# Attention and a two-layer MLP on one core: the second matrix product by one level of Strassen's scheme on 12 of 16 inner blocks, with its weight decoded earlier

## The chip, the core and the metric

The kernel runs on one core of a Trainium2 chip. The metric is the device time of one launch in microseconds (us). In the text, PE is the matrix engine (TensorE), PEld its weight loads, DVE is VectorE, ACT is ScalarE, POOL is GpSimd, and SP is the engine from whose queue nearly every DMA is issued. Every engine takes its own instructions strictly in order; an instruction that waits holds up all that stand behind it on its engine.

## What is computed

Causal attention with 4 batches, 12 heads, 448 positions and head dimension 64, then an MLP on 1792 tokens of width 768, with 2048 inner features:

```python
scores = scale * q @ k.T                      # q, k, v: (4, 12, 448, 64) float32
scores = where(triu(ones, k=1), -1e9, scores)
p = exp(scores - max); p = p / (sum(p) + 1e-9)
x = (p @ v).transpose(0, 2, 1, 3).reshape(1792, 768)
h = x @ w_in                                  # first product, (768, 2048)
g = where(h >= 1, h, where(h <= -1, 0, (h + 1) ** 2 / 4))
out = g @ w_out                               # second product, (2048, 768)
```

The two weights arrive as 64-bit floats. The kernel sees them as pairs of 32-bit words and rebuilds float32 numbers from them.

## The kernel before

All work is entered as tasks of a list (`Plan`), each with one engine or several to choose from, its costs, and the buffers that it reads and writes. `Plan.solve` (L145) orders the PE tasks by nominal times that the program gives them, derives due times for all others, and runs a greedy schedule over nine pairs of settings and five rounds each; the best of them is written out as the instruction order of each engine. So a change in the tasks moves instructions on every engine, and the order on each engine is fixed when the program is built.

Numbers are carried as two parts: a rounded part ("hi") and the rest ("lo"). One product is three matmuls, hi by hi, hi by lo and lo by hi (`PASSES`, L479).

**Weights.** `decode` (L429) brings a block of 128 rows and 384 numbers in: one DMA of 384 KB into a staging tile, one ACT pass over the high words (L449), two DVE passes that put the float together (L452, L454), then the hi part as a copy (ACT, POOL or DVE, L413 and L415) and the lo part as a subtraction (POOL or DVE, L423 and L422). Each of the 16 slices f of a weight has two such blocks, called halves here. `w_in` is decoded while the first pairs of heads go through attention, `w_out` when the tiles of `w_in` come free, from 373 us on.

**Attention.** 24 pairs of heads follow one another (`prep_pair`, `prep_v`, `pair`): loads of q and k, a transpose on DVE (L577), scores on PE, minimum and exponential on DVE and ACT (L718, L722), transposes on PE (L657), and the product with v (L747). Matmuls of the first product (`mlp1`, L481) for the batch before are woven in between, 20 steps in each of the first four pairs of a batch, few in the fifth and none in the sixth.

**First product.** `mlp1` takes 18 matmuls of 448 columns for one slice of 128 inner features and one batch, then one ACT pass (L497), two DVE passes (L500, L506) for the function g, and a store into the DRAM scratch `g_scratch` (L510). After the last pair of heads only these matmuls are left for PE, from 373 to 420 us.

**Second product.** `TILES` (L330) cuts the 14 blocks of 128 tokens into groups of 4, 4, 3, 2 and 1. For each group the loop over the 16 slices f loads g back (`gr`), splits it into hi and lo (`gs`, ACT L413 and DVE L422), and issues for each token block six matmuls of 384 columns (L836): 3 passes by 2 halves of the output. 14 blocks x 16 slices x 6 are 1344 matmuls. The sums stay in PSUM (`a` with 5 buffers, `h` with 3) until the last slice, and are then copied out (L851, L855) and stored.

```python
both = [(c, m) for m in range(3) for c in range(2)]
nc.tensor.matmul(out=acc[t, c][:, :NO], lhsT=gs[:, a, (t - t0) * P:(t - t0 + 1) * P],
                 rhs=wo[f][:, z, c * NO:(c + 1) * NO], ...)
```

Of the kernel before, what the change touches and what calls it, by code (L numbers as in the profile page):

```python
# [303 lines left out]
def kernel(  # L304
# [9 lines left out]
    nc = tc.nc  # L314
# [15 lines left out]
    TILES = (4, 4, 3, 2, 1)  # L330
    GT = max(TILES)
# [13 lines left out]
        "w": KF, "st": 2, "wm": 2, "x": 9, "r": 3, "vv": 1, "h": 3,  # L345
# [3 lines left out]
        "gr": 4, "gs": 4, "ot": 2, "a": 5,  # L349
# [31 lines left out]
    mask2 = const.tile([P, 3 * P], F32, name="mask2")  # L381
# [6 lines left out]
    for i in range(NI):  # L388
        e = const.tile([P, P * (i // 2 + 1)], F32, name=f"e{i}")
        if i % 2 == 0:  # L390
            nc.gpsimd.memset(e[:, T * (i + 1):], 0.0)
        es.append(e)
    qb = [const.tile([P, 2, 2, T], F32R, name=f"qb{n}") for n in range(2)]
    zero = const.tile([P, 512], F32R, name="zero")
# [34 lines left out]
    def decode(w, c, src, prio, no):  # L429

        if no < 2 * (KF - NSTG):
            st, z = stages[no // 2 % NSTG], no % 2
            raw = lambda: st.tile.bitcast(U32)[:, z]
        else:
            st, z = buf("st", [P, 2 * S]), 0
            raw = lambda: st.tile.bitcast(U32)[:, :DM]
        m = buf("wm", [P, W2])

        def words(t):
            return raw().rearrange("p (c t) -> p c t", t=2)[:, :, t]  # L440

        def mu():
            return m.tile.bitcast(U32)

        hi = lambda: w[:, 0, c * W2:(c + 1) * W2]
        lo = lambda: w[:, 1, c * W2:(c + 1) * W2]
        dst, ap = src
        dma_task(lambda: dst(raw()), lambda: ap, dma(P * DM * 4), 0.38, writes=[(st, (z, 0)), (st, (z, 1))] + ([] if z or st in stages else [(w, ("to", c))]))
        task([("ACT", act(W2, 0.04), lambda: nc.scalar.activation(  # L449
            out=m.tile, in_=words(1).bitcast(F32), func=ACTF.Prelu, scale=W_SHIFT, alpha=W_SIGN))],  # L450
            prio, reads=[(st, (z, 1))], writes=[(m, 0)])
        task([("DVE", dve(W2, True), lambda: nc.vector.tensor_scalar(  # L452
            out=mu(), in0=mu(), scalar1=3, scalar2=None, op0=ALU.logical_shift_left), True)], prio, writes=[(m, 0)])
        task([("DVE", dve(W2) + 0.08, lambda: nc.vector.scalar_tensor_tensor(  # L454
            out=mu(), in0=words(0), scalar=29, in1=mu(), op0=ALU.logical_shift_right, op1=ALU.bitwise_or), True)],
            prio, reads=[(st, (z, 0))], writes=[(m, 0)])
        task(copy_alts(hi, lambda: m.tile, W2, "ACT POOL DVE"), prio, reads=[(m, 0)], writes=[(w, (0, c))])
        task(sub_alts(lo, lambda: m.tile, lambda: hi().bitcast(F32), W2, "POOL DVE"),
             prio, reads=[(m, 0), (w, (0, c))], writes=[(w, (1, c))])
# [4 lines left out]
    def load_w_in(f, prio):  # L464
        w = wi[f] = buf("w", [P, 2, DM], F32R)
        for c in range(2):
            src = w_in[c * K2 * P:(c + 1) * K2 * P, f * 2 * P:(f + 1) * 2 * P]
            decode(w, c, (lambda t: t.rearrange("p (k c) -> p k c", k=K2),
                          src.rearrange("(k p) c -> p k c", p=P)), prio, 2 * f + c)

    def load_w_out(f, prio):
        w = wo[f] = buf("w", [P, 2, DM], F32R)
        for c in range(2):
            decode(w, c, (lambda t: t, w_out[f * P:(f + 1) * P, c * DM:(c + 1) * DM]), prio, 2 * KF)
# [422 lines left out]
```

## Time and profile before

| What | Value |
|---|---|
| median of three timed runs | 659.58 us (658.79 to 660.16) |
| span of the profiled execution, first to last instruction | 657.8 us (no other time of that execution is given) |
| mean granted PE clock | 0.997 of full |
| PE busy | 637.1 us, 97% |
| DVE, ACT, POOL busy | 343.5, 334.9, 183.0 us |
| chain that ended last | PE 79%, DMA 8%, DVE 5%, ACT 3% |
| matmuls of the first product | 1152, of the second 1344 |

A row of the engine groups gives the engine, the operation, the tiles, the count, the busy time, the mean duration in ns, and then the idle time just before. Matmul durations overlap, so the spacing of starts in the timeline tells the rate of PE, not the mean duration.

### The profile page before, as it was taken

What the parts mean: (1) busy time and instruction counts of PE and PEld (TensorE: products, weight loads), DVE (VectorE), ACT (ScalarE), POOL (GpSimd) and SP (SyncE); (2) the same over time, 40 slices, a digit from 0 to 9 for tenths busy, and PEclk for the clock granted to TensorE, in tenths of its full rate; (3) what the DMA queues carried; (4) which work ended last, traced back from release to release, by engine and by line L of the source; (5) the groups of instructions that cost most, each with busy time, mean ns of one, the idle gap of its engine ahead of it and who ended that gap; (6) DMA issues with size and microseconds to landing.
All of it is one profiled execution on the core that took longest, in us unless ns stands there. A gap on an engine that the chain in (4) does not pass through costs nothing.

```text
span 657.8 us, 11550 instructions
## 1 busy us (share of the span) xinstructions
PE 637.1 (97%) x3782; PEld 558.6 (85%) x3782; DVE 343.5 (52%) x857; ACT 334.9 (51%) x877; POOL 183.0 (28%) x322
## 2 busy tenths in 40 slices
PE   7989999999898999999999999999999999999997
PEld 3447798887697888798887699999999999999997
DVE  4867787867666565665644476655532112112221
ACT  3879979757746556846555533444431112112122
POOL 3657665443412222612212133334310000000000
PEclk8999999999999999999999999999999999999999
DMA  9889999677776655756442465666642214213221
GB/s 220 227 240 228 234 264 275 190 214 204 195 230 187 168 148 154 180 171 178 101 128 62 156 214 159 199 195 195 196 160 65 64 49 145 73 49 109 72 84 49
DMA packets 91900, 105.75 MB, mean 161 GB/s; under 512 B 34368, under 2 KB 75840, under 8 KB 91840
## 3 DMA queue, kind: packets, MB, share of 16 engines
q1 hardware_dynamic: 91600, 104.46, 57.2%
q10 hardware_dynamic: 240, 0.55, 0.4%
q8 instruction: 30, 0.49, 0.3%
q14 instruction: 30, 0.25, 0.2%
HBM read 67.35 MB, written 20.19 MB: 133 GB/s over the span
## 4 chain that ended last, share of the span: by engine, by line
PE 79%; DMA 8%; DVE 5%; ACT 3%; SPq 2%; issue 2%; POOL 1%; DVEq 0%; ACTq 0%; POOLq 0%
PE h L488 29%; PE a L836 27%; PE h L836 9%; PE t L657 5%; PE t L747 4%; DMA st<-in_k_dram 4%; PE s L700 3%; SPq L405 2%; DMA st<-in_q_dram 2%; PE s L695 1%; DVE qs L577 1%; ACT e L722 1%; PE s L704 1%; DVE s L718 1%; DMA w<-in_moe_w_in_dram 1%
## 5 line engine op out<-in xcount | busy, mean ns | idle before, releaser
L488 PE MATMUL h<-x,w 128*128 128x448 f32 x1152 | 264.4, 372 | 2.2 <-DVE x L422 1.0
L488 PEld LDWEIGHTS h<-x,w 128*128 128x128 f32 x1152 | 208.5, 188 | 19.1 <-DVE x L422 2.2
L836 PE MATMUL a<-w,gs 128*128 128x384 f32 x1008 | 197.7, 334 | 0.0
L836 PEld LDWEIGHTS a<-w,gs 128*128 128x128 f32 x1008 | 176.8, 188 | 0.1
L422 DVE TENSOR_TENSOR gs<-gr,gs 128x512 fp32r<-128x512 f32 (+3 forms) x79 | 45.3, 574 | 139.3 <-ACT gs L413 135.1
L413 ACT ACTIVATE gs<-gr 128x512 fp32r<-128x512 f32 (+3 forms) x78 | 38.8, 500 | 137.4 <-PE h L836 103.5
L722 ACT ACTIVATE e<-s,mn 128x256 f32<-128x256 f32 (+6 forms) x168 | 80.8, 485 | 35.7 <-DVE mn L718 33.3
L718 DVE CUSTOM_DVE_ANT_0 s<-s,mask 128x256 f32<-128x256 f32 (+6 forms) x168 | 73.2, 453 | 45.8 <-PE s L700 22.7
L423 POOL TENSOR_TENSOR w<-wm,w 128x384 fp32r<-128x384 f32 x64 | 67.3, 1052 | 65.3 <-ACT w L413 64.0
L836 PE MATMUL h<-w,gs 128*128 128x384 f32 x336 | 80.7, 334 | 0.0
L657 PE MATMUL t<-ident,e 128*128 128x128 f32 x384 | 61.9, 279 | 5.7 <-DVE x L422 4.1
L679 ACT ACTIVATE pt<-t 128x512 f32<-128x512 f32 (+2 forms) x138 | 59.9, 466 | 4.4 <-PE t L657 3.1
L642 POOL TENSOR_SCALAR e<-e,su 128x256 f32<-128x256 f32 (+6 forms) x92 | 51.9, 569 | 35.3 <-DVE su L733 29.3
L657 PEld LDWEIGHTS t<-ident,e 128*128 128x128 f32 x384 | 44.1, 140 | 20.6 <-issue 5.8
L836 PEld LDWEIGHTS h<-w,gs 128*128 128x128 f32 x336 | 60.3, 188 | 0.0
L500 DVE TENSOR_TENSOR vv<-h,r 128x448 f32<-128x448 f32 x64 | 39.7, 620 | 36.4 <-ACT r L497 35.7
L497 ACT ACTIVATE r<-h,half 128x448 f32<-128x448 f32 x64 | 40.0, 632 | 36.2 <-PE h L488 35.4
L577 DVE STREAM_TRANSPOSE qs<-st 128x448 f32<-128x448 f32 x48 | 45.8, 966 | 22.1 <-DMA st<-in_q_dram 12.4
L747 PE MATMUL t<-pt,vr 128*64 128x448 f32 (+3 forms) x384 | 50.3, 391 | 0.6 <-ACT pt L679 0.6
L728 POOL TENSOR_SCALAR su<-su 128x2 f32<-128x2 f32 (+1 forms) x72 | 19.5, 270 | 107.9 <-ACT e L722 106.0
L747 PEld LDWEIGHTS t<-pt,vr 128*64 128x64 f32 (+1 forms) x384 | 23.2, 135 | 30.9 <-issue 21.5
L506 DVE SCALAR_TENSOR_TENSOR r<-r,vv 128x448 f32<-128x448 f32 x64 | 45.5, 711 | 1.3
(54 smaller groups left out, 506.4 us busy)
## 6 DMA issues: line engine op xcount, KB each, us to landing
g_scratch<-r SPq DMA_DIRECT2D x64, 224.0 KB, 2.4
st<-in_moe_w_out_dram SPq DMA_DIRECT2D x32, 384.0 KB, 3.4
w<-in_moe_w_in_dram SPq DMA_DIRECT2D x28, 384.0 KB, 4.8
st<-in_k_dram SPq DMA_DIRECT2D x94, 108.0 KB, 3.0
st<-in_q_dram SPq DMA_DIRECT2D x93, 108.0 KB, 3.0
q<-tt SPq DMA_DIRECT2D x76, 128.0 KB, 2.4
gr<-g_scratch SPq DMA_DIRECT2D x32, 256.0 KB, 2.7
k<-ks SPq DMA_DIRECT2D x76, 96.0 KB, 2.2
```

Of the source, the lines that this page charges most:

```text
L422: "DVE": ("DVE", dve(n), lambda: nc.vector.tensor_tensor(out=dst(), in0=x(), in1=y(), op=op), port),
L423: "POOL": ("POOL", pool_tt(n), lambda: nc.gpsimd.tensor_tensor(out=dst(), in0=x(), in1=y(), op=op), True),
L488: nc.tensor.matmul(out=h[:, :S], lhsT=wi[f][:, a, kk * P:(kk + 1) * P], rhs=x[:, c], start=(kk == 0 and n == 0), stop=(kk == KD - 1 and n ...
L506: task([("DVE", dve(S), lambda: nc.vector.scalar_tensor_tensor(out=r.tile, in0=r.tile, scalar=1.0, in1=y.tile, op0=ALU.min, op1=ALU.mult), ...
L577: task([("DVE", 0.81, lambda g=g, t=t: nc.vector.transpose(out=x[:, g].rearrange("p (r c) -> p c r", c=C), in_=t.tile.rearrange("p (c d) - ...
L642: ("POOL", pool_ts(n, 0.09), lambda: nc.gpsimd.tensor_scalar(out=ev(), in0=ev(), scalar1=sc(), scalar2=1.0, op0=ALU.mult, op1=ALU.mult), T ...
L657: nc.tensor.transpose(t[:, c:c + P], es[i][:, j * P:(j + 1) * P], ident)
L679: task([("ACT", act(n), lambda: nc.scalar.activation(out=dst(), in_=src(), func=ACTF.Copy)), ("DVE", dve(n), lambda: nc.vector.tensor_copy ...
L718: task([("DVE", dve(n) + 0.01, lambda s=s, n=n, i=i: nc.vector.tensor_tensor_reduce(out=s[:, :n], in0=s[:, :n], in1=mask2[:, 3 * P - n:] i ...
L722: task([("ACT", act(n, 0.19), lambda s=s, n=n, i=i: nc.scalar.activation(out=es[i][:, :n], in_=s[:, :n], func=ACTF.Exp, scale=-1.0, bias=m ...
L747: nc.tensor.matmul(out=o[64 * g:64 * g + 64, j * P:S], lhsT=vr[:k, j, g, :], rhs=pt[:k, 7 * j:5 * j + NI, g, :], start=(j == 0), stop=(j = ...
L836: nc.tensor.matmul(out=acc[t, c][:, :NO], lhsT=gs[:, a, (t - t0) * P:(t - t0 + 1) * P], rhs=wo[f][:, z, c * NO:(c + 1) * NO], start=(f == ...
```

## The change

**Second product.** The tokens are now taken in 7 pairs of blocks (`token_pair`), the inner slices in 8 pairs. For the first two pairs of slices (four slices, "plain") everything is as before: 8 products of three matmuls for a pair. For the other six pairs, a 2 x 2 by 2 x 2 block product is made with 7 products in place of 8 (Winograd's form of Strassen's scheme). That needs four sums of 128 x 128 blocks of g for each token pair (`sums`), hi and lo of 7 blocks in place of 4, and on the weight's side 7 tiles of hi and lo ("units") in place of 4, with four differences of halves (`minus`), once for the whole kernel. The 8 sums in PSUM (all 8 banks, 5 in `a`, 3 in `h`) are combined on the way out: one copy, nine additions, two stores of 384 KB; the last token pair does the plain slices last and stores four quarters of 192 KB.

**Weight.** The halves of slices 0 to 11 of `w_out`, 24 in all, are decoded during attention, from the eighth pair of heads on, two behind each pair, and parked as float32 in a DRAM scratch `w_scratch` by a store of 192 KB each. From 373 us on they are loaded from there, and only the 8 halves of slices 12 to 15 are still decoded then. 50 units are made, each with one hi copy and one lo subtraction.

**Buffers.** Constants of attention lie in a pool that closes with it; the weight tiles are units of half the size (32 in `w`, 9 in `w2` that opens after attention, 9 in `w3` that opens after the last store of g); the zero tile of the filling matmuls is a buffer of `k2`.

```diff
-    def decode(w, c, src, prio, no):
+    def decode(m, raw, src, writes=(), behind=(), after=()):
...
+    def narrow_w_out(f, c, behind):
+        m = small("wm", buf)
+        raw_out(f, c, m, raw_in(buf("sr", [P, DM])), behind=behind)
+        dma_task(lambda: w_dram[f, c], m[2], dma(P * W2 * 4), 0.35, reads=[m[:2]], writes=[(wkeys, (f, c))])
+
+    def out_half(f, c, m, units):
+        claim = [(u, "to") for u in units]
+        after = last + (tails if any(u.tag == "w3" for u in units) else [])
+        if f >= NARROW:
+            raw_out(f, c, m, raw_in(buf("st", [P, 2 * S])), claim, after=after)
+        else:
+            dma_task(m[2], lambda: w_dram[f, c], dma(P * W2 * 4), 0.35, reads=[(wkeys, (f, c))],
+                     writes=[m[:2]] + claim, after=after)
...
+    def load_w_out_pair(f):
...
+        out_half(f, 0, m11, [w["11"]])
+        split(m11, w["11"])
+        out_half(f, 1, m12, [w["T1"], w["T3"]])
+        minus(m12, m11, m11)
+        split(m11, w["T1"])
+        out_half(f + 1, 1, m22, [w["22"], w["T2"]])
+        minus(m22, m12, m12)
+        split(m12, w["T3"])
+        split(m22, w["22"])
+        minus(m22, m11, m22)
+        split(m22, w["T2"])
+        out_half(f + 1, 0, m21, [w["21"], w["T4"]])
+        split(m21, w["21"])
+        minus(m21, m22, m21)
+        split(m21, w["T4"])
...
+    for n in range(2 * NARROW):
+        narrow_w_out(n // 2, n % 2, [attn_tasks[7 + n // 2]])
...
+        def product(x, z, lhsT, unit, reads):
...
+                for n, (a, c) in enumerate(PASSES):
+                    nc.tensor.matmul(out=acc[x][:, :NO], lhsT=lhsT(a), rhs=unit[:, c],
+                                     start=(start and n == 0), stop=(stop and n == 2))
...
+        def sums(z):
+            for x, y, d, op in ((1, 3, 4, ALU.add), (0, 1, 1, ALU.subtract), (4, 0, 5, ALU.subtract), (2, 5, 6, ALU.subtract)):
...
+        for f, fast in groups:
+            z, hl = bbuf("z", [P, 7 * P]), bbuf("hl", [P, 2, 7 * P], F32R)
...
+            if fast:
+                for x in ORDER:
+                    i, name = BLOCK[x]
+                    product(x, z, lambda a, hl=hl, i=i: hl[:, a, i * P:(i + 1) * P], wo[f][name], both)
...
+        take("1", "1a")
+        add("6", "1a", "2a")
+        add("2", "1a", "1a")
+        add("3", "2a", "1b")
...
+        store(0, 0, DM, [0, 1])
+        store(1, 0, DM, [0, 1])
```

Lines move: the ACT pass of the decode is L446, the DVE passes L449 and L451, hi copies L418 and L420, lo and differences L427 and L428, matmuls of the first product L565, of the second L950.

Three places show how the order of the instructions moves. A row is line, operation, out<-in tiles, shape, and how many follow one another.

PE, the turn from the first product to the second, before (a and h are PSUM sums, w the weight, gs the split g):

```order
L488 MATMUL h<-x,w 128x448 x237
L836 MATMUL a<-w,gs 128x384 x6
L488 MATMUL h<-x,w 128x448 x3
L836 MATMUL a<-w,gs 128x384 x6
L488 MATMUL h<-x,w 128x448 x3
L836 MATMUL a<-w,gs 128x384
```

The same engine in the change, from the end of the first token pair on (w_5583 to w_5609 are units of the last pair of slices, w_4811 to w_4888 are plain units that the second token pair takes):

```order
L950 MATMUL a<-w_5489,hl 128x384 x3
L950 MATMUL h<-w_5528,hl 128x384 x3
L950 MATMUL a<-w_5583,hl 128x384 x3
L950 MATMUL h<-w_5529,hl 128x384 x3
L950 MATMUL h<-w_5584,hl 128x384 x3
L950 MATMUL a<-w_5608,hl 128x384 x3
L950 MATMUL a<-w_4811,hl 128x384 x3
L950 MATMUL a<-w_4813,hl 128x384 x3
L950 MATMUL a<-w_4821,hl 128x384 x3
L950 MATMUL a<-w_4826,hl 128x384 x3
L950 MATMUL a<-w_4888,hl 128x384 x3
L950 MATMUL a<-w_5609,hl 128x384 x3
```

The run of 237 matmuls before the turn is still there with the same length; the product with the last unit, w_5609, now stands behind five products of the next token pair.

DVE just after attention, before (wm is the decoded half, vv and r belong to the function g, gs is g split):

```order
L500 TENSOR_TENSOR vv<-h,r 128x448
L506 SCALAR_TENSOR_TENSOR r<-r,vv 128x448
L422 TENSOR_TENSOR gs<-gr,gs 128x512
L452 TENSOR_SCALAR wm<-wm 128x384
L454 SCALAR_TENSOR_TENSOR wm<-st,wm 128x384
```

DVE in the change, the last rows ahead of that last unit (sr, wm and st hold halves, hl the split g, ot the output):

```order
L427 TENSOR_TENSOR w_5529<-wm,w_5529 128x384
L427 TENSOR_TENSOR w_5584<-sr,w_5584 128x384
L427 TENSOR_TENSOR w_5608<-sr,w_5608 128x384
L427 TENSOR_TENSOR hl<-z,hl 128x512
L427 TENSOR_TENSOR ot<-h,ot 128x384
L427 TENSOR_TENSOR ot<-a,ot 128x384 x2
L427 TENSOR_TENSOR ot<-h,ot 128x384 x2
L427 TENSOR_TENSOR w_5609<-sr,w_5609 128x384
```

Lo parts that POOL made before are now mostly on DVE, and the last lo part of a unit stands behind the first output additions.

SP during the third batch of attention, before (st takes q and k, tt and ks are copies of them, r is g):

```order
L405 DMA st<-in_q_dram 32x864
L405 DMA g_scratch<-r 128x448
L405 DMA st<-in_k_dram 32x864 x4
L405 DMA g_scratch<-r 128x448 x2
L405 DMA q_3780<-tt 64x2x256 x4
L405 DMA g_scratch<-r 128x448
```

SP in the change at the same place:

```order
L410 DMA st<-in_q_dram 32x864
L410 DMA g_scratch<-r 128x448
L410 DMA st<-in_k_dram 32x864 x4
L410 DMA sr<-in_moe_w_out_dram 128x768
L410 DMA w_scratch<-wm 128x384
L410 DMA g_scratch<-r 128x448 x2
L410 DMA sr<-in_moe_w_out_dram 128x768
L410 DMA q_3891<-tt 64x2x256 x4
L410 DMA g_scratch<-r 128x448
L410 DMA k_3918<-ks 64x384 x4
L410 DMA w_scratch<-wm 128x384
```

A load of a raw half and the store of the decoded half stand in the queue between the loads of attention; in 18 of the 24 cases the store is the very next DMA behind its own load.

## Rows read from the trace of the kernel before

**Rows 1.** Page, part 1: busy us, share of the span, instructions of PE.
```profile
PE 637.1 (97%) x3782; PEld 558.6 (85%) x3782; DVE 343.5 (52%) x857; ACT 334.9 (51%) x877; POOL 183.0 (28%) x322
```

**Rows 2.** Windows: us, busy of PE, PEld, DVE, ACT, POOL; granted clock, DMA share, GB/s.
```profile
373.00:420.00 47.00, 47.00 (x232) 43.62 (x233) 34.06 (x55) 19.44 (x36) 17.61 (x19) 1.00 0.63 190
420.00:450.00 30.00, 30.00 (x173) 29.90 (x173) 17.25 (x30) 13.71 (x26) 9.94 (x11) 1.00 0.63 191
450.00:654.00 204.00, 203.68 (x1176) 203.36 (x1174) 55.08 (x104) 49.38 (x103) 11.89 (x12) 1.00 0.31 97
```

**Rows 3.** Timeline of PE in the second product: start, us, what.
```profile
419.29 1.23 PE L836 MATMUL a<-w,gs 128*128 128x384 f32 x6
...
449.68 2.41 PE L836 MATMUL a<-w,gs 128*128 128x384 f32 x13
451.93 0.33 PE L836 MATMUL h<-w,gs 128*128 128x384 f32 x1
```

**Rows 4.** The chain of waits, its longest piece: start, us, what.
```profile
372.98 46.47 PE h L488 x228
```

**Rows 5.** Windows of attention, columns as in rows 2.
```profile
70.00:110.00 40.00, 39.46 (x235) 33.44 (x234) 30.87 (x80) 32.16 (x84) 22.77 (x35) 1.00 0.99 265
...
190.00:208.00 18.00, 16.54 (x97) 13.54 (x95) 12.20 (x32) 8.90 (x25) 2.94 (x8) 1.00 0.81 223
...
172.00:373.00 201.00, 196.99 (x1209) 162.90 (x1207) 113.60 (x315) 119.89 (x339) 52.12 (x114) 1.00 0.59 158
```

**Rows 6.** The decode's second DVE pass from 70 to 110 us: count, duration.
```profile
L454 DVE SCALAR_TENSOR_TENSOR wm<-w,wm x10: 541/550/823, 81.3 to 108.7; 128x384 uint32<-128x384 uint32 x10
```

**Rows 7.** Groups by shape over the span: busy, mean ns, idle before and its releaser.
```profile
L422 DVE TENSOR_TENSOR gs<-gr,gs 128x384 fp32r<-128x384 f32 x16 | 8.9, 558 | 42.4 <-ACT gs L413 42.4
L422 DVE TENSOR_TENSOR gs<-gr,gs 128x128 fp32r<-128x128 f32 x16 | 4.7, 292 | 14.0 <-ACT gs L413 14.0
L423 POOL TENSOR_TENSOR w<-wm,w 128x384 fp32r<-128x384 f32 x64 | 67.3, 1052 | 65.3 <-ACT w L413 64.0
L415 POOL TENSOR_SCALAR w<-wm 128x384 fp32r<-128x384 f32 x16 | 8.5, 532 | 22.3 <-DVE wm L454 20.3 <-PE h L488 1.8
L449 ACT ACTIVATE wm<-st 128x384 f32<-128x384 f32 x36 | 19.3, 546 | 5.5 <-DMA st<-in_moe_w_out_dram 3.2 <-POOL w L423 1.9
```

**Rows 8.** Timeline of DVE and POOL just after attention.
```profile
373.69 0.62 DVE L500 TENSOR_TENSOR vv<-h,r 128x448 f32<-128x448 f32 x1
374.35 0.62 DVE L506 SCALAR_TENSOR_TENSOR r<-r,vv 128x448 f32<-128x448 f32 x1
374.60 1.53 POOL L423 TENSOR_TENSOR gs<-gr,gs 128x512 fp32r<-128x512 f32 x1 [8.98 <-ACT gs L413]
374.89 1.79 DVE L422 TENSOR_TENSOR gs<-gr,gs 128x512 fp32r<-128x512 f32 x1
...
377.79 0.68 DVE L422 TENSOR_TENSOR gs<-gr,gs 128x512 fp32r<-128x512 f32 x1
378.39 0.35 DVE L452 TENSOR_SCALAR wm<-wm 128x384 uint32<-128x384 uint32 x1
378.77 0.56 DVE L454 SCALAR_TENSOR_TENSOR wm<-st,wm 128x384 uint32<-128x384 uint32 x1
379.25 0.35 DVE L452 TENSOR_SCALAR wm<-wm 128x384 uint32<-128x384 uint32 x1
...
380.10 2.63 POOL L423 TENSOR_TENSOR w<-wm,w 128x384 fp32r<-128x384 f32 x2
...
381.77 0.61 DVE L500 TENSOR_TENSOR vv<-h,r 128x448 f32<-128x448 f32 x1
```

**Rows 9.** DMA issues: count, KB each, median us from issue to landing.
```profile
st<-in_moe_w_out_dram SPq DMA_DIRECT2D x32, 384.0 KB, 3.4
gr<-g_scratch SPq DMA_DIRECT2D x32, 256.0 KB, 2.7
```

**Rows 10.** Timeline of the last instruction before the last store lands.
```profile
654.08 0.36 ACT L858 ACTIVATE ot<-a 128x224 f32<-128x224 f32 x1 [0.39 <-DVE ot L855]
```

More of the change, by code (lines that the diff above doesn't have):

```diff
@@ L392 @@
         es.append(e)
[L393 to L394 removed]
+    qb = [early.tile([P, 2, 2, T], F32R, name=f"qb{n}") for n in range(2)]
     half = const.tile([P, 1], F32, name="half")
@@ L454, in decode @@
         task([("DVE", dve(W2) + 0.08, lambda: nc.vector.scalar_tensor_tensor(
             out=mu(), in0=words(0), scalar=29, in1=mu(), op0=ALU.logical_shift_right, op1=ALU.bitwise_or), True)],
[L456 to L459, printed above, removed]
+            0.0, reads=[(rb, (rk, 0))], writes=[(mb, mk)])
@@ new lines, in split, with raw_in, small @@
+    def split(m, u, names="DVE POOL"):
+        mb, mk, mt = m
+        hi, lo = (lambda: u[:, 0]), (lambda: u[:, 1])
+        task(copy_alts(hi, mt, W2, "ACT POOL DVE"), 0.0, reads=[(mb, mk)], writes=[(u, 0)])
+        task(sub_alts(lo, mt, lambda: hi().bitcast(F32), W2, names),
+             0.0, reads=[(mb, mk), (u, 0)], writes=[(u, 1)])
+    def raw_in(st):
+        return st, 0, lambda: st.tile.bitcast(U32)[:, :DM]
+    def small(tag, make):
+        m = make(tag, [P, W2])
+        return m, 0, lambda: m.tile
@@ L471, in load_w_out @@
[L471 to L474, printed above, removed]
+            if f < KF - NSTG:
+                raw, claim = raw_in(stages[(2 * f + c) % len(stages)]), []
+            else:
+                raw, claim = raw_in(buf("st", [P, 2 * S])), [(u, "to")]
+            m = small("wm", buf)
+            decode(m, raw, (lambda t: t.rearrange("p (k c) -> p k c", k=K2),
+                            src.rearrange("(k p) c -> p k c", p=P)), claim)
@@ new lines, in halves, with unit, load_w_out @@
+    def halves(tag, n):
+        st = buf(tag, [P, 2 * S if tag == "st" else DM])
+        return [(st, z, lambda z=z: st[:, z * W2:(z + 1) * W2]) for z in range(n)]
+    def unit():
+        n = state["units"]
+        state["units"] += 1
+        if n < slots["w2"]:
+            return bbuf("w2", [P, 2, W2], F32R)
+        if n < slots["w2"] + slots["w"]:
+            return buf("w", [P, 2, W2], F32R)
+        return lbuf("w3", [P, 2, W2], F32R)
+    def load_w_out(f):
+        wo[f] = [unit() for _ in range(2)]
+        for c, (u, m) in enumerate(zip(wo[f], halves("st", 2))):
+            out_half(f, c, m, [u])
+            split(m, u)
@@ new lines, in load_w_out_pair, with minus @@
+    def load_w_out_pair(f):
+        w = wo[f] = {}
+        for n in ("11", "T1", "T3", "22", "T2", "21", "T4"):
+            w[n] = unit()
+        if f in (6, 10):
+            m11, m12, m22, m21 = halves("st", 2) + halves("st", 2)
+        else:
+            m11, m12, m22, m21 = small("wm", buf), small("wm", buf), *halves("sr", 2)
+        def minus(x, y, dst):
+            task(sub_alts(dst[2], x[2], y[2], W2, "DVE POOL"),
+                 0.0, reads=[q[:2] for q in (x, y) if q is not dst], writes=[dst[:2]])
+        out_half(f, 0, m11, [w["11"]])
[13 more added lines that the diff above has]
+        split(m21, w["T4"])
@@ L787 @@
             mlp1(b, f, M_AT[b])
[L788 to L791 removed]
+    state = {"b": False, "l": False, "units": 0}
     def open_b():
[L794 to L795 removed]
+        if not state["b"]:
+            state["b"] = True
             attn.close()
[L797 removed]
+            open_pools(base, "w2 z hl")
             open_pools(base, "a", PSUM)
[L800 to L806 removed]
@@ new lines, in open_l, with late, make_buf, make @@
+    def open_l():
+        if not state["l"]:
+            state["l"] = True
+            mid.close()
+            open_pools(base, "w3 ot", side="right")
+    last, tails = attn_tasks[-HP:], g_tasks[-KF:]
+    def late(opener):
+        def make_buf(tag, shape, dtype=F32):
+            def make():
+                opener()
+                return pools[tag].tile(shape, dtype, tag=tag, name=tag)
+            return plan.buf(tag, make)
+        return make_buf
+    bbuf, lbuf = late(open_b), late(open_l)
@@ L865 @@
+    for m in range(NTT // 2):
+        token_pair(m)
     with tc.manual_schedule():
```

241 lines of the change are left out of this document (132 added, 109 removed).

## The prediction

> **What bounds the kernel now.** I read the engine totals first, then the windows by stage, then the timelines of PE, DVE and POOL around the turn from the first product to the second. PE is busy 637.1 of 657.8 us [rows 1], and the windows say where the rest is lost: all of it in attention. From 373 us, when the last pair of heads is through, PE has no gap until the end, 47.00 of 47.00, 30.00 of 30.00 and 203.68 of 204.00 us, at the full granted clock of 1.00, which is the higher of its two levels, 2.4 GHz [rows 2]. In these stages only fewer or shorter matmuls can save time. DVE has room there as long as the weight is being decoded (34.06 of 47 us, 17.25 of 30), and a great deal afterwards (55.08 of 204) [rows 2]. From 172 to 373 us, where the change puts new work, PE idles 4.0 us, with DVE at 57%, ACT at 60% and DMA at 0.59 [rows 5].
>
> The rate of the second product comes from the timeline: 13 matmuls start between 449.68 and 451.93 us [rows 3], 0.173 us each. The mean duration of a group would mislead here, since matmuls overlap. The first product takes 46.47 us for 228 matmuls of its last run [rows 4], 0.204 each.
>
> **The sum.** The parts are priced on the span of the profiled execution, 657.8 us. The median of the runs, 659.58, is 1.8 above it, and I carry this 1.8 over.
>
> *Matmuls removed.* Before, 14 blocks x 16 slices x 6 make 1344. Now a token pair takes 2 plain groups x 24 and 6 groups x 21, 174 together, and 7 pairs 1218. So 126 fall away, times 0.173: **-21.8 us**. Shape and number of columns stay the same, and three matmuls in a row into one sum are no new pattern: the first product does that with 18 and runs 448 columns in 0.204, the same 2.2 columns a ns as 384 in 0.173. What remains is whether PE can be fed without gaps.
>
> *Steady state, token pairs 2 to 7.* A pair takes PE 174 x 0.173 = 30.1 us. On DVE stand, for a pair, six lo parts of 896 elements, two of 512, some 20 block sums of 128 and some 9 additions of 384. The durations of 128 and 384 elements are 292 and 558 ns [rows 7], so 133 for each further 128, and about 1.09 us for 896. That is 6.5 + 1.4 + 5.8 + 5.0 = 18.7 us beside 30.1: hidden. ACT has nine wide copies of a similar size, about 8 us. One group from its load on takes 2.7 us for the DMA of the same 256 KB [rows 9], about 1.2 for four sums, 1 for hi and 1.1 for lo, with some waits 7 us; with three buffers it has three group times, 3 x 3.6. At a pair's end, PE begins the next pair with the sums 2, 3, 4 and 8, whose PSUM tiles are the first to be read out, and needs the others 8.3 us later. **0 us**; if DVE came late there, each pair boundary would cost about one addition, 0.6, six times 3.6 at most.
>
> *The turn, 373 to about 455 us.* This is the tight place. During the last run of the first product and the first token pair, all 50 units and 24 differences have to be made, where before 32 halves were decoded, which left DVE a quarter free. In the order of the changed program, DVE has, from there to the last unit (the one that PE now takes behind five products of the second pair): 16 and 16 passes of the function g, 9 and 9 of the decode, 62 subtractions of 384, 6 of 896, 4 of 512, 22 of 128, 5 additions. From start to start DVE takes 0.66 and 0.54 us for the two passes of g, 0.60 for 512 elements, and 0.38 and 0.48 for the decode [rows 8]; start to start is 0.08 below the duration, so I take 0.48 for 384, 1.01 for 896, 0.21 for 128, 0.5 for an addition. The sum is 10.6 + 8.6 + 7.7 + 29.8 + 6.1 + 2.4 + 4.6 + 2.5 = 72.3 us. On POOL stand meanwhile 12 subtractions of 384 at 1.05 and 6 copies at 0.53 [rows 7], 4 more of other sizes for about 3 us: 18.8 us.
>
> These get in each other's way. A DVE subtraction of 512 takes 0.68 alone and 1.79 beside a POOL subtraction of 1.53 [rows 8], so 1.1 of 1.53 is lost, 0.7. A pass that reads the product's PSUM tile is not lengthened, 0.61 with POOL busy [rows 8]; such work is a fifth of the 72.3. So 0.7 x 0.8 x 18.8 = 10.8 us, and DVE would be through at 373 + 83.1 = 456.1 us.
>
> PE wants that unit at: second product begins at 419.29 [rows 3], six matmuls of the first in between 1.2, all products of the pair but one 171 x 0.173 = 29.6, five products of the next pair 2.6: 452.7 us. The difference is a stall of **+3.4 us**. The ends are 0 (no interference: through at 445.3) and +11.4 (POOL's 18.8 wholly lost: 464.1). A slip of attention moves both times alike. The nine units of `w3` also wait for the last store of g: some 4.5 us after the last matmul of the first product (two passes of g on DVE 1.2, one on ACT about 0.6, a landing near 2.7 [rows 9]), so near 426, and their raw halves land 3.4 us after issue [rows 9]; that leaves over 20 us, so this wait is not the later one. I take the measured loss and no waits of DVE itself; before, DVE often waited in this stage, but now there is nearly always some other work in its queue.
>
> By the Trainium skill (SBUF — State Buffer, Who interferes with whom) a DVE instruction with two SBUF inputs and a GpSimd instruction that reads SBUF share a port that is locked for a whole instruction. Rows 8 agree in kind; the loss they show is 0.7 of the POOL time and not all of it. With a full lock this term would be nearer 11.4 than 3.4.
>
> *Attention.* 24 halves move ahead of 373 us. Each adds on DVE 0.38 + 0.48, on ACT 0.55 [rows 7], on SP two issues, and 576 KB of DMA. In the 201 us from 172 on that is 21 us of DVE (57 to 67%), 13 of ACT (60 to 66%), and 13.8 MB, some 69 GB/s on top of 158 [rows 5]. The stretch from 70 to 110 us is the nearest: ten halves in 40 us [rows 6], twice the density, with hi and lo parts besides, at 265 GB/s and a DMA share of 0.99, and there PE loses 0.5 us [rows 5]. Against that stands 190 to 208, where loads of q and k come late and PE loses 1.5 of 18 us [rows 5]; if all eleven such stretches went that way, 16 in place of 4, it would be +12. I take **+2 us**, nearer to the first, with the ends 0 and +12. The decode of the first weight changes its order, but not its work: 0, with 2 us either way.
>
> *The end.* The last instruction before the last store is an ACT pass of 0.36 us that had waited 0.39 for DVE [rows 10]; now it is one addition of 384 on DVE, 0.56, and a store of the same 192 KB. **0 us**, within 0.3.
>
> Together: -21.8 + 3.4 + 2 = -16.4. The span would be 641.4, the median 659.6 - 16.4 = **643.2 us**.
>
> **The rivals.**
>
> *The whole gain.* Neither the turn nor attention costs anything: 659.6 - 21.8 = 637.8 (637 to 640.5). For it: PE lost nothing in the turn before, and 0.5 in the densest stretch. Against it: the sum of DVE is already above what PE allows.
>
> *The lock is full.* DVE loses POOL's whole time in the turn: 659.6 - 21.8 + 2 + 11.4 = 651.2 (647 to 654). For it: POOL was placed there in subtractions, the kind that clashed. Against it: the row of 0.61 and the 0.7. This is what the sentence on the skill's rule would give.
>
> *SP is held up in attention, and the kernel gets slower.* A store of a parked half has to wait on SP until its load has landed (3.4 us [rows 9]) and the three passes are through (0.55 + 0.38 + 0.48): 4.8 us, and in 18 of 24 cases it is the next DMA behind that load. Everything behind it, the loads of q and k and the stores of g, waits too, and PE's order is fixed. If each of the 18 costs PE what late loads cost it from 190 to 208, 1.5 us, that is 26: 659.6 - 21.8 + 26 = 664. It decides from 1.2 us for each store on. For it: these late loads are in the trace before. Against it: loads are issued a pair ahead, and SP has gaps that the order uses.
>
> **How the numbers follow.** Chances: the forecast's case (640.5 to 647) 0.48, the whole gain 0.25, the full lock or a like stall (647 to 654) 0.15, held-up SP with a time above before 0.07, and what lies between, 654 to 658, 0.02, about equal 0.03. A measurement of this kernel can tell 0.2%, 1.3 us. Faster 0.90, same 0.03, slower 0.07. The range from 637.5 to 652 holds the forecast's case, most of the whole gain, and the full lock as computed.
>
> **What would show it.** In the profile after: 1218 matmuls of the second product at 0.173 spacing; from about 455 us to the end PE without gaps. In the turn: DVE near 95% busy from 375 to 455, its subtractions lengthened wherever POOL runs, and PE waiting on a DVE subtraction into a weight unit, 3 us in total. In attention: the last run of the first product starting at about 375 in place of 373, POOL as before, DVE and ACT some 20 and 13 us busier. The forecast is wrong if the last run starts after 380 (then the SP queue shows waits of several us in front of the parked stores), if PE idles over 7 us in the turn, or if PE has gaps at the boundaries of token pairs.

## The result, and the profile after

The change takes 640.58 us (median of 4 runs, 639.97 to 643.76) against 659.49 in the same series before: 18.9 us less, ratio 0.9704 with a 95% interval of 0.9669 to 0.974. The profiled execution took 639.97 us, its span is 638.2; before, the span was 657.8. The spans differ by 19.6 us.

The windows of the changed kernel, cut as in [rows 2] and [rows 5] (length, busy us and count of PE, PEld, DVE, ACT, POOL, granted clock, DMA share, GB/s):

```profile
172.00:373.00 201.00, 196.67 (x1214) 163.57 (x1213) 129.39 (x359) 128.21 (x356) 59.62 (x123) 1.00 0.79 216
373.00:420.00 47.00, 46.82 (x235) 43.55 (x234) 45.40 (x84) 24.29 (x49) 15.32 (x15) 1.00 0.61 193
420.00:450.00 30.00, 29.88 (x170) 29.15 (x168) 26.96 (x56) 15.12 (x28) 6.12 (x6) 1.00 0.60 180
...
419.95:634.68 214.73, 213.59 (x1225) 212.23 (x1223) 129.39 (x281) 61.36 (x87) 32.72 (x38) 1.00 0.33 102
```

The last row runs from the first matmul of the second product to the last one; before, the same stretch went from 419.29 to 653.69:

```profile
419.29:653.69 234.40, 234.39 (x1351) 233.97 (x1349) 72.49 (x133) 63.77 (x130) 21.83 (x22) 1.00 0.36 110
```

So, between these two executions, the whole gain lies in the second product: 234.40 us became 214.73. It begins 0.66 us later than before, and between its last matmul and the end of the span there are 3.5 us in place of 4.1. 0.66 - 19.67 - 0.6 gives the -19.6.

Attention from 172 to 373 us carries its new work almost unnoticed: DVE 129.39 in place of 113.60 us, ACT 128.21 in place of 119.89, 216 GB/s in place of 158, and PE busy 196.67 in place of 196.99 [rows 5].

PE's loss in the second product stands in the timeline of the weight loads around the end of the first token pair. The weight loads run a little ahead of their matmuls, so their row shows a wait more fully than PE's (in brackets the idle time before a row and what ended it):

```profile
448.57 0.19 PEld L950 LDWEIGHTS a<-w,hl 128*128 128x128 f32 x1
449.15 0.30 PEld L950 LDWEIGHTS a<-w,hl 128*128 128x128 f32 x2 [0.39 <-DVE w L427]
449.44 0.19 PEld L950 LDWEIGHTS h<-w,hl 128*128 128x128 f32 x1
450.83 0.84 PEld L950 LDWEIGHTS h<-w,hl 128*128 128x128 f32 x5 [1.20 <-DVE w L427]
451.65 3.33 PEld L950 LDWEIGHTS a<-w,hl 128*128 128x128 f32 x19
455.48 2.57 PEld L950 LDWEIGHTS a<-w,hl 128*128 128x128 f32 x15 [0.50 <-DVE w L427]
```

Three waits of 2.1 us in all, each ended by a lo subtraction (L427) into a unit of the weight. After 455 us nothing else is lost: no row of PE has a gap up to the end. The DVE timeline of the same place has the last unit:

```profile
453.94 1.02 DVE L427 TENSOR_TENSOR ot<-h,ot 128x384 f32<-128x384 f32 x2
454.88 0.55 DVE L427 TENSOR_TENSOR w<-sr,w 128x384 fp32r<-128x384 f32 x1
```

It is through at 455.43; PE takes it at 455.48. From 373 to 420 us DVE is busy 45.40 of 47 us, where it was 34.06 [rows 2]. From 373 to 455.4 it is busy 77.62 of 82.4 us. Nearly half of the 4.8 us in which it stands still are waits for ACT's pass over the raw halves that are still decoded here (waits of DVE from 373 to 456: total, how many, longest):

```profile
DVE wm L449 <- ACT wm L446: 1.2, 2, 0.8
DVE sr L449 <- ACT sr L446: 1.0, 1, 1.0
```

What POOL costs DVE can be read there too. 14 of DVE's 149 instructions take longer than others of their shape that run while POOL is idle, each of the 14 while POOL is busy, and together they lose 6.7 us, 0.27 of the 24.6 us that POOL is busy. The same subtraction with POOL's 1.37 us of 375.74 beside it, and alone:

```profile
376.15 1.51 DVE L427 TENSOR_TENSOR hl<-z,hl 128x512 fp32r<-128x512 f32 x1
380.18 0.68 DVE L427 TENSOR_TENSOR hl<-z,hl 128x512 fp32r<-128x512 f32 x1
```

### The profile page after: what moved, and what is told of

It reads as the page before. It is cut to its first block, busy times and chain, and to the rows that moved or that the text cites. A ratio compares the mean times of both kernels' runs of the same rounds, so it can differ in the third digit from the quotient of the medians.

```text
span 638.2 us, 11607 instructions
## 1 busy us (share of the span) xinstructions
PE 616.9 (97%) x3656; PEld 537.4 (84%) x3656; DVE 434.8 (68%) x1081; ACT 340.5 (53%) x851; POOL 206.6 (32%) x351
## 4 chain that ended last, share of the span: by engine, by line
PE 65%; DVE 11%; DMA 9%; ACT 4%; issue 4%; SPq 3%; POOL 3%; ACTq 0%; DVEq 0%; POOLq 0%
PE h L565 25%; PE a L950 19%; PE h L950 9%; PE t L734 4%; PE t L824 4%; DMA st<-in_q_dram 3%; SPq L410 3%; PE s L777 2%; DVE w L427 2%; DVE qs L654 1%; ACT e L799 1%; DVE s L795 1%; DMA sr<-in_moe_w_out_dram 1%; DMA st<-in_k_dram 1%; PE s L781 1%
## 5 line engine op out<-in xcount | busy, mean ns | idle before, releaser
L565 PE MATMUL h<-x,w 128*128 128x448 f32 x1152 | 260.2, 369 | 2.3 <-DVE vv L577 1.3
L565 PEld LDWEIGHTS h<-x,w 128*128 128x128 f32 x1152 | 208.5, 188 | 15.8 <-DVE vv L577 1.9
L950 PE MATMUL a<-w,hl 128*128 128x384 f32 x840 | 160.3, 335 | 0.3 <-DVE w L427 0.2
L950 PEld LDWEIGHTS a<-w,hl 128*128 128x128 f32 x840 | 147.0, 188 | 1.0 <-DVE w L427 0.9
L418 ACT ACTIVATE hl<-z 128x896 fp32r<-128x896 f32 (+1 forms) x54 | 47.0, 870 | 126.9 <-PE h L950 82.9
L427 DVE TENSOR_TENSOR hl<-z,hl 128x896 fp32r<-128x896 f32 (+1 forms) x55 | 56.3, 1024 | 71.9 <-ACT hl L418 71.9
L795 DVE CUSTOM_DVE_ANT_0 s<-s,mask 128x256 f32<-128x256 f32 (+6 forms) x168 | 72.7, 454 | 30.4 <-PE s L772 15.8
L950 PE MATMUL h<-w,hl 128*128 128x384 f32 x378 | 79.4, 335 | 0.9 <-DVE w L427 0.9
L719 POOL TENSOR_SCALAR e<-e,su 128x256 f32<-128x256 f32 (+5 forms) x105 | 60.1, 579 | 31.7 <-DVE su L810 24.6
L950 PEld LDWEIGHTS h<-w,hl 128*128 128x128 f32 x378 | 66.8, 188 | 1.2 <-DVE w L427 1.2
L734 PEld LDWEIGHTS t<-ident,e 128*128 128x128 f32 x384 | 43.6, 140 | 21.2 <-issue 6.2
L756 ACT ACTIVATE pt<-t 128x256 f32<-128x256 f32 (+2 forms) x137 | 59.1, 466 | 4.1 <-PE t L734 3.3
L428 POOL TENSOR_TENSOR z<-z 128x128 f32<-128x128 f32 x26 | 18.6, 720 | 128.1 <-DMA z<-g_scratch 126.9
```

The lines of the kernel that those rows point to most:

```text
L418: "ACT": ("ACT", act(n, 0.04), lambda: nc.scalar.activation(out=dst(), in_=src(), func=ACTF.Copy)),
L427: "DVE": ("DVE", dve(n), lambda: nc.vector.tensor_tensor(out=dst(), in0=x(), in1=y(), op=op), port),
L565: nc.tensor.matmul(out=h[:, :S], lhsT=wi[f][kk // K2][:, a, kk % K2 * P:(kk % K2 + 1) * P], rhs=x[:, c], start=(kk == 0 and n == 0), stop= ...
L719: ("POOL", pool_ts(n, 0.09), lambda: nc.gpsimd.tensor_scalar(out=ev(), in0=ev(), scalar1=sc(), scalar2=1.0, op0=ALU.mult, op1=ALU.mult), T ...
L734: nc.tensor.transpose(t[:, c:c + P], es[i][:, j * P:(j + 1) * P], ident)
L756: task([("ACT", act(n), lambda: nc.scalar.activation(out=dst(), in_=src(), func=ACTF.Copy)), ("DVE", dve(n), lambda: nc.vector.tensor_copy ...
```

## The experiments

The change was timed first, then twelve runs in four series, one of them the change again, each beside its own runs of the kernel before. The table gives the ratio to these; the start and length of the second product are from each profiled execution. "Loss" is the length less its matmuls at 0.1733 us (their spacing before, taken from 500 to 600 us) and less 0.204 us for each matmul of the first product that lies in it: six in most runs, nine in the plain kernel and with 16 or 32 early halves, three with 14 of 16 and 32 early.

| Kernel | us | ratio (95%) | starts at | length | loss |
|---|---|---|---|---|---|
| before | 659.49 | 1 | 419.29 | 234.40 | 0.3 |
| the change, 12 of 16 | 640.58 | 0.9704 (0.9669 to 0.974) | 419.95 | 214.73 | 2.4 |
| the change again | 639.89 | 0.9678 (0.9634 to 0.9722) | 416.78 | 214.78 | 2.5 |
| loads in order | 641.70 | 0.9722 (0.9694 to 0.975) | 422.55 | 214.55 | 2.2 |
| plain, 0 of 16 | 661.47 | 1.0013 (0.9995 to 1.0031) | 422.66 | 234.96 | 0.2 |
| 8 of 16 | 646.54 | 0.9823 (0.9769 to 0.9877) | 419.56 | 221.64 | 2.1 |
| 16 early halves | 650.79 | 0.9874 (0.9834 to 0.9915) | 425.64 | 224.45 | 11.5 |
| early work doubled | 717.04 | 1.0857 (1.0814 to 1.0899) | 423.61 | 288.50 | 76 |
| units on DVE only | 642.93 | 0.9728 (0.9695 to 0.9762) | 420.23 | 216.64 | 4.3 |
| two split buffers | 641.29 | 0.9718 (0.9673 to 0.9762) | 417.72 | 216.12 | 3.8 |
| 14 of 16 | 649.22 | 0.9825 (0.9785 to 0.9865) | 425.46 | 220.14 | 11.5 |
| 32 early halves | 660.86 | 1.0000 (0.998 to 1.002) | 421.13 | 234.37 | 21 |
| 14 of 16, 32 early | 659.81 | 0.9982 (0.9957 to 1.0008) | 424.88 | 229.69 | 22 |
| last slices parked | 646.58 | 0.9784 (0.975 to 0.9819) | 424.15 | 219.51 | 7.2 |

**No Strassen at all.**

```diff
-    NPLAIN = 2
+    NPLAIN = 8
...
-        first_use = "16234758" if final else "23481675"
+        first_use = "2348"
...
+        for x, n in (("2", "1a"), ("3", "1b"), ("4", "2a"), ("8", "2b")):
+            take(x, n)
```

> All 16 slices go through the plain path (8 products for a token pair), 1344 matmuls in the second product; early decode, parking in DRAM and the new buffers stay. Theory (the gain is the 126 matmuls at 0.173 us, nothing else): back by 21.8 us less the 1.3 us that PE now loses in the turn, so 640.6 + 20.5 = 661, 659 to 662, no faster than the kernel before. Rival (early decode or the new buffers bring part of the gain by themselves): clearly under the kernel before, 650 to 656.

661.47 us, as the theory had it. The second product is as long as before, and PE has no gap in it:

```profile
422.66:657.62 234.96, 234.96 (x1354) 234.50 (x1352) 53.18 (x87) 45.77 (x83) 5.38 (x9) 1.00 0.31 91
```

So early decode, parking and the new buffers bring nothing by themselves; the gain is the 126 matmuls.

**8 of 16.**

```diff
-    NPLAIN = 2
+    NPLAIN = 4
```

> Four plain pairs of slices in place of two: 8 of 16 slices by Strassen. 42 more matmuls x 0.173 = 7.3 us, 6 units and 8 differences fewer to make in the turn. Theory (matmul count alone decides, the turn loses about 1 us and gets that back): 640.6 + 7.3 - 1 = 647, 646 to 648.5. Rival (DVE work in the turn costs time well beyond the PE gaps that were seen): under 645, since 14 fewer passes of 0.48 us on DVE are 7 us.

646.54, within what the theory gave (646 to 648.5); three of the four runs lie within 0.14 us, the fourth at 652.43. The 42 more matmuls are 7.3 us; the length grew by 6.9. But the part of the theory by which the turn would give its loss back did not come true: the loss is still 2.1 us, with 14 passes fewer on DVE. Here DVE itself waits, for the last raw halves to be brought in, and then a subtraction beside POOL takes 1.63 us in place of 0.55 (timeline of DVE):

```profile
444.24 0.36 DVE L449 TENSOR_SCALAR sr<-sr 128x384 uint32<-128x384 uint32 x1 [2.14 <-ACT sr L446]
444.64 0.56 DVE L451 SCALAR_TENSOR_TENSOR sr<-st,sr 128x384 uint32<-128x384 uint32 x1
...
446.30 1.63 DVE L427 TENSOR_TENSOR w<-sr,w 128x384 fp32r<-128x384 f32 x1
```

PE's longest wait is for a split of g that stands behind these on DVE (timeline of the weight loads):

```profile
449.93 0.30 PEld L950 LDWEIGHTS a<-w,hl 128*128 128x128 f32 x2 [1.40 <-DVE hl L427]
```

So PE can lose the same 2 us where DVE's sum of work does not explain it: DVE is busy 68.54 us from 373 to 456, where it is 78.22 in the change.

**Fewer early halves, and its control.** For the second product the loads of halves follow one another (`chain`); this alone is the control. The plain kernel, the doubled early work and both kernels with 14 of 16 have it too.

```diff
-    NARROW = KF - 4
+    NARROW = 8
...
+        n0, behind = len(plan.tasks), list(chain)
...
+        chain[:] = [plan.tasks[n0]]
```

> Early decode for slices 0 to 7 only, so 16 halves decoded and parked, 16 decoded in the turn (8 more than in the change). The loads of halves in the turn are also made to follow one another in order. Theory (DVE is the bound of the turn, with no room): 8 x 0.86 us more on DVE, PE loses 5 to 7 us more there, attention gives back under 1: 645 to 648. Rival (DVE had room, or PE can go on with other products): 640 to 642.

> Control for the run with fewer early halves: the change with only the loads of halves in the turn made to follow one another in order. Theory and rival: as the change, 639.5 to 642.5; what differs is how far a new order of the same work moves the time.

The control is the change: 641.70, loss 2.2. With 16 early halves the time is 650.79, more than the theory's 645 to 648. The profiled execution, 655.38, is the slowest of the four: its second product starts 3.1 us later than the control's (425.64 against 422.55) and is 9.9 us longer. Only the second of these can be put down to the halves; the repeat below moves the start by as much with no change at all. Two windows:

```profile
440.00:460.00 20.00, 16.31 (x85) 14.26 (x83) 19.17 (x42) 11.22 (x20) 3.49 (x5) 0.99 0.57 168
460.00:480.00 20.00, 18.12 (x83) 15.71 (x84) 16.47 (x40) 7.38 (x12) 4.38 (x6) 0.84 0.34 112
```

One of the waits in them, in PE's timeline:

```profile
460.68 1.60 PE L953 MATMUL h<-w,hl 128*128 128x384 f32 x3 [1.80 <-ACT w L418]
```

The waits come one after another between 451 and 470 us, and in their wake the granted clock falls: 0.84 on the mean from 460 to 480, while 83 matmuls take the place of 115. The three matmuls of the last row need 1.60 us, where three in the change take 0.68. The theory had the direction and the DVE sum (6.9 us more). The weight loads stand still for 10.1 us here and for 1.8 in the control, 8.3 more; the remaining 1 us of the longer loss goes with matmuls at the lower clock, which the theory had left out. 5.3 of the 10.1 us end with a hi copy on ACT and not with DVE.

**Early work doubled.**

```diff
+        dma_task(lambda: w_dram[KF + f, c], m[2], dma(P * W2 * 4), 0.35, reads=[m[:2]], writes=[(wkeys, (KF + f, c))])
+        m = small("wm", buf)
+        raw_out(f, c, m, raw_in(buf("sr", [P, DM])), behind=behind)
```

> Every early half is decoded and stored twice (the first copy goes to a scratch that nothing reads): 24 more raw loads of 384 KB, stores of 192 KB, ACT passes, pairs of DVE passes, all during attention. Loads in the turn follow one another in order. Theory (attention is bound by PE and takes this work up in gaps; the first 24 halves cost it about 1 us): +1 to +4 us on the change. Rival (parked stores hold up SP, and so the loads of q and k): 1.2 us or more for each store, +20 us and more.

717.04 us: far off for the theory, and yet not the rival. The second product begins at 423.61, the control's at 422.55. But attention did not take 24 more halves: 31 of the 48 are parked by 373 us, where the control has 23 of its 24. So the run shows that eight more parked stores cost attention about 1 us, and not what 24 more would. The loss is all afterwards. SP's timeline:

```profile
443.48 0.33 SPq L410 DMA_DIRECT2D sr<-in_moe_w_out_dram  x1
443.86 0.43 SPq L410 DMA_DIRECT2D w_scratch<-wm  x1
448.76 0.33 SPq L410 DMA_DIRECT2D sr<-in_moe_w_out_dram  x1
```

PE's timeline, its longest wait:

```profile
476.93 1.60 PE L956 MATMUL a<-w,hl 128*128 128x384 f32 x3 [43.62 <-ACT w L418]
```

Early halves go one by one through a single staging tile (`sr`), and with nothing else in the way one takes 5.3 us (443.48 to 448.76): load, ACT pass, DVE passes, and only then the next load. 48 of them were not through before 475 us, and PE stood still for 43.6 us waiting for a unit. In the change the last of 24 is parked at 373.4 us, when attention has just ended. The early decode has an end of its own, and halves that come after it hold PE up. That 24 is the most that attention can take is not shown: 31 were through by 373 us here.

**Units on DVE only.**

```diff
-    def split(m, u, names="DVE POOL"):
+    def split(m, u, names="DVE"):
...
-            task(sub_alts(dst[2], x[2], y[2], W2, "DVE POOL"),
+            task(sub_alts(dst[2], x[2], y[2], W2, "DVE"),
```

> Subtractions of 384 elements for units of the second weight and their differences may go to DVE only, not to POOL. DVE gets 12 more at 0.48, 5.8 us, and loses no time to POOL in the port. Theory (POOL takes from DVE about 0.7 of its own time, 10.8 us in the turn): DVE is through as early or some us earlier, PE loses 0 to 1 us in the turn: 639.5 to 641.5. Rival (POOL's help is worth its work): DVE 5 us later, PE loses 5 us more: 644 to 647.

642.93 lies between the two, and the run does not tell them apart: the planner gave POOL other two-input work in exchange. From 373 to 456 us POOL now makes 18 block sums of g (5 in the change), 636 ns each; DVE is busy 77.39 us there (78.22 in the change), and the last unit comes at 457.75 in place of 455.43, though PE does not wait for that one: its last wait ends at 453.26. POOL still lengthens DVE's instructions, by 4.2 us beside 18.9 us of POOL. The weight loads stand still for 2.8 us, 0.7 more than in the change; most of the other 1.2 us of loss goes with a granted clock of 0.91 from 440 to 460 us, where the change has 1.00. The group of POOL's block sums in this stretch, the last unit in DVE's timeline, and the window:

```profile
L428 POOL TENSOR_TENSOR z<-z 128x128 f32<-128x128 f32 x18 | 11.2, 636 | 6.2 <-DVE z L427 3.7 <-DMA z<-g_scratch 1.6 <-DVE sr L427 0.8
```

```profile
457.21 0.54 DVE L427 TENSOR_TENSOR w<-sr,w 128x384 fp32r<-128x384 f32 x1
```

```profile
440.00:460.00 20.00, 18.64 (x94) 17.20 (x94) 19.75 (x46) 8.62 (x15) 4.55 (x7) 0.91 0.37 114
```

**14 of 16, and its control.**

```diff
-    NPLAIN = 2
+    NPLAIN = 1
...
-        "w2": 9, "z": 3, "hl": 3, "w3": 9, "ot": 3, "a": 5,
+        "w2": 11, "z": 3, "hl": 2, "w3": 10, "ot": 3, "a": 5,
```

> One plain pair of slices in place of two: 14 of 16 slices by Strassen, 53 units (11 in the pool that opens after attention, 10 in the last), two buffers of split g in place of three to make room. 21 matmuls fewer x 0.173 = 3.6 us; three units and four differences more in the turn, 7 passes of 0.48 on DVE = 3.4 us. Theory (DVE bounds the turn, PE the rest): the two cancel, 639 to 642. Rival (the turn has room): 637 to 638. If two buffers are too few, later pairs show gaps on PE.

> Control for 14 of 16: the change with two buffers of split g in place of three. A buffer is held from the hi copy to the last product, about 1 + 1.1 + 0.5 + 3.6 = 6.2 us, and two give 7.2: theory: no cost, 640 to 642. Rival (two are too few as soon as DVE is late, at each end of a token pair): 1 to 3 us at each of six pair ends, 646 and more.

Two buffers of split g cost about 1 us at most (641.29, loss 3.8). 14 of 16 is 8 us slower than that, with 21 matmuls fewer: the theory's 639 to 642 was far too good. PE loses 3.6 of 20 us from 440 to 460, the clock is 0.84 from 460 to 480, as with 16 early halves. Why three more units and four more differences cost that much is not shown.

**All halves early, with 12 and with 14 of 16.**

```diff
-    NARROW = KF - 4
+    NARROW = KF
...
-        narrow_w_out(n // 2, n % 2, [attn_tasks[7 + n // 2]])
+        narrow_w_out(n // 2, n % 2, [attn_tasks[6 + n // 3]])
```

> All 16 slices of the second weight are decoded early (32 halves, three behind a pair of heads, from the seventh pair on) and loaded back. Theory (the one staging tile for early halves lets one through per 5.3 us at best, and in the order of the program eight stores still stand behind the first loads of g): the last halves are parked after 373 us, DVE has as much to do in the turn as before, and time is the change's or a little more, 640 to 645. Rival (the turn is relieved of 8 x 0.86 us on DVE): PE loses nothing there, 638 to 639.

> 14 of 16 slices by Strassen as before, with all 32 halves decoded early. 21 matmuls fewer than the change, 3.6 us. Theory (DVE bounds the turn, and is not relieved, since the last halves come late): as 14 of 16 before, 646 to 651. Rival (the decode in the turn was what was too much): 637 to 641.

The whole gain is gone: 660.86 and 659.81, as before the change. That eight halves are parked after 373 us is as expected, the price is not. (The doubled run had parked 31 by then, this one 24, so the staging tile's 5.3 us is not the only limit; the order of the program is another.) The last half is parked at 425.8 us in the first of the two, and while the staging tile works through the last eight, DVE gets little of its own work for the turn: 32.20 us from 373 to 420 in place of 45.40.

```profile
373.00:420.00 47.00, 46.34 (x229) 42.89 (x230) 32.20 (x66) 16.94 (x32) 4.21 (x5) 1.00 0.68 218
420.00:440.00 20.00, 16.58 (x82) 15.22 (x81) 13.93 (x26) 9.00 (x17) 0.00 (x0) 0.93 0.69 213
440.00:460.00 20.00, 12.25 (x56) 9.89 (x55) 19.01 (x41) 11.91 (x24) 3.21 (x2) 0.84 0.31 98
```

What DVE has not done by 420 it does with PE waiting, and the granted clock goes down. In the second kernel, with 14 of 16, PE loses 6.5 us from 440 to 460 at the full clock, and the clock falls only in the next stretch, where a single wait is 4.5 us long:

```profile
440.00:460.00 20.00, 13.50 (x58) 9.39 (x57) 20.00 (x43) 12.25 (x25) 8.33 (x1) 1.00 0.45 136
460.00:480.00 20.00, 14.31 (x63) 12.98 (x63) 17.51 (x36) 6.48 (x12) 8.73 (x12) 0.83 0.31 97
```

**The last slices parked in place of the first.**

```diff
-        if f >= NARROW:
+        if f < KF - NARROW:
...
-        narrow_w_out(n // 2, n % 2, [attn_tasks[7 + n // 2]])
+        narrow_w_out(KF - NARROW + n // 2, n % 2, [attn_tasks[7 + n // 2]])
```

> As many halves parked as in the change (24), but those of slices 4 to 15; the 8 that are decoded in the turn are now those of the plain slices 0 to 3, which the second product takes first and for which units are free from 373 us on. DVE has the same sum of work in the turn. Theory that DVE's sum alone makes the 2.1 us of PE idle in the turn: no change, the weight-load row idle 2 to 3 us from the first to the last matmul of the second product. Rival (the late chain makes it: raw halves of the last slices may be loaded only after the last store of g, and land, are decoded and subtracted one after another): the idle time falls under 1 us, 1.5 to 2 us faster than the change, 637.5 to 640 if attention comes out alike. A third way: the plain units come later, and PE waits at 420 us in place of 450.

646.58, worse than the change, loss 7.2. The raw halves of the plain slices go through the two `wm` tiles here. The late raw halves are gone, and it does not help: raw halves now come first, DVE is busy only 37.06 of the 47 us from 373 to 420, and three waits of PE follow at 453 to 456 us, one of them for POOL. The weight loads stand still for 4.2 us, and the granted clock is 0.90 from 440 to 460 and 0.93 from 460 to 480. The window, and this wait in PE's timeline:

```profile
373.00:420.00 47.00, 45.44 (x233) 41.20 (x229) 37.06 (x76) 21.91 (x42) 9.43 (x11) 1.00 0.68 217
```

```profile
455.21 0.44 PE L950 MATMUL a<-w,hl 128*128 128x384 f32 x1 [1.62 <-POOL w L420]
```

Both ways of putting it were too simple. DVE's sum is the same as in the change, and the time is not; nor is it the late chain alone.

**The change once more.**

> The changed kernel once more, unaltered, to see how far the start of the second product and the loss in the turn move from run to run, without a new order of the instructions. Theory: 639.5 to 643, the second product begins at 419 to 422 us, the weight-load row is idle 2.5 us from there to the last matmul.

```profile
416.78:631.56 214.78, 213.61 (x1225) 212.26 (x1223) 129.06 (x281) 61.31 (x87) 32.41 (x38) 1.00 0.34 102
```

The length of the second product is the same to 0.05 us, 214.78 and 214.73. Its start is not: 416.78 and 419.95, with the same program. Two of the 3.2 us arise between 66 and 82 us, where the granted clock fell in the first execution and did not in the second. The windows from 70 to 110 us, the first execution above:

```profile
70.00:110.00 40.00, 38.54 (x222) 31.40 (x222) 34.73 (x85) 31.14 (x82) 22.48 (x34) 0.96 0.93 246
70.00:110.00 40.00, 38.78 (x233) 32.57 (x232) 35.10 (x86) 32.19 (x86) 23.32 (x36) 1.00 0.97 258
```

Everything that attention loses or gains within 3 us is within this.

## Why the prediction was right

The forecast was 643.2 us with a range of 637.5 to 652; it came to 640.58. By its own steps, on the spans:

*Matmuls removed, -21.8.* Held. The second product has 1218 matmuls, and with none left out (the plain kernel) the time goes back to 661.47. With 8 of 16, 84 are gone in place of 126, and the ratio is 0.9823.

*Steady state, 0.* Held: PE has no gap after 455 us, at none of the six pair boundaries. DVE is busy 53% of the time there (90.99 of 170 us from 460 to 630), where the sum of 18.7 in 30.1 us had 62%.

*The turn, +3.4.* Right in place and kind, 2.1 measured (loss 2.4 less the 0.3 of before). The working fits as it was set up: PE would have wanted the last unit at 419.95 + 1.2 + 29.6 + 2.6 = 453.4 us and got it at 455.48; the two earlier waits, 1.6 us, are a part of the same 2.1. But that DVE's end came out within 0.7 us, 455.4 where the working gave 456.1, is luck, since its parts do not hold. POOL cost DVE 6.7 us and not 10.8: 0.27 of POOL's time, where the working had 0.57 (0.7 where both engines read SBUF twice). DVE stood still for 4.8 us, where the working took no waits. Its own work was 70.9 us where the working had 72.3. POOL was busy 24.6 us and not 18.8. A full lock on the whole of POOL's time would have been 464. The run that was to take POOL out did not. 8 of 16 loses the same 2 us with DVE 9.7 us less busy, by a wait of DVE and a subtraction lengthened beside POOL.

*Attention, +2.* Mis-sized, if anything: 0.66 in the profiled execution, -2.5 in the repeat. It can't be told from nothing; the 0.66 holds about 2 us of the fall of the clock near 75 us, which the profile before does not have. From 172 to 373 us DVE is 15.8 us busier and ACT 8.3, where the working had some 20 and 13. The nearest stretch, 70 to 110 us [rows 5], was the right one to go by; the row of 190 to 208, which gave the +12, was not.

*The end, 0.* -0.6, twice the 0.3 that was allowed for. Where it comes from is not shown; before, the last store waited for ACT's pass behind DVE's [rows 10].

*Rivals.* The whole gain would have been 637.8, and came within 3 us; the repeat has single runs from 636.84. The full lock did not come. The SP rival had the waits right in kind and their price wrong. SP does stand in front of parked stores, waiting for DVE's second pass: in the change from 160 to 375 us ten times, 20.6 us in all and 4.0 at the longest (4.8 each was reckoned), and with the early work doubled, from 120 to 480 us (total, how many, longest):

```profile
SPq L410 <- DVE wm L451: 51.9, 31, 4.4
```

Yet the second product starts 0.66 us later than before in the one and 1.1 later than the control's in the other, where 1.2 us for each of the eight stores that attention took on top would have been 9.6. A likely reason is that the loads behind a waiting store are not due yet; that is not shown.

What the prediction did not see at all is how narrow the place is. It took the early decode as work moved into gaps for 2 us. The runs show an upper and a lower edge: 16 early halves cost 9 us more than 24 (650.79 against the control's 641.70), and 32 cost 21 more (660.86 against 639.89 in the same series).

## What to carry to other kernels

Where one engine has no gaps, fewer instructions on it count in full, and the question is only who has to prepare its operands and when; make that sum for the engine next in line, over the stretch up to the moment when the operand is wanted, with start-to-start times. Then look at the supply of that engine as well: much the same sum of DVE work cost 2, 7 or 21 us here, and it was the less the more of it DVE could do in the first 47 us (45.40, 37.06 and 32.20 us). A serial chain through one buffer has a rate of its own (5.3 us a half with nothing else in the way), and what it has not delivered when the stage ends, the next stage waits for.

## What was not expected of the hardware

- After a row of short waits of PE the granted clock can fall: to a mean of 0.84, which is a third of the stretch at 1.2 GHz and the rest at 2.4, from 460 to 480 us with 16 early halves and with 14 of 16. During the wait of 43.6 us it is at 0.50, and 0.74, 0.60 and 0.81 in the three stretches of 20 us after 480. The sum of the waits does not tell whether it falls: with two split buffers the weight loads stand still for 3.4 us and it stays at 1.00, with the units on DVE only for 2.8 us and it is 0.91; with 14 of 16 and 32 early halves PE loses 6.5 of 20 us at 1.00. Where it falls, the loss is 1 to 4 us more than the waits; in the doubled run it is some 10 us more.
- The same program begins its second product 3.2 us apart in two executions (416.78 and 419.95), and its length differs by 0.05. Two of the 3.2 us go with a fall of the clock in attention that one execution has and the other has not; the rest comes in small steps in attention, and its cause is not shown.
- DVE loses only a part of the time that POOL works beside it: 0.27 of POOL's busy time in the turn, 0.22 with the units on DVE only. In the other direction, with 14 of 16 and 32 early halves one block sum of 128x128 on POOL, 0.56 us on the mean in the change, took 8.33 us by the profile, in a stretch where DVE was busy 20.00 of 20 us; no run tests whether DVE was the cause.

What stays open: how the 2.1 us that PE still loses divide between DVE's sum and the late halves. The 2.2 us in which DVE waits for late raw halves are as long as the loss, but the run that parked them in place of the first slices lost more, and neither it nor 8 of 16 settles it.
